# Relu-squared attention and a GELU MLP on one core: q and k rows in a ring of four groups, v in a ring of seven, PSUM tiles handed out by the kernel, a new order of the work

## The chip, the core and the metric

One NeuronCore of a Trainium2 chip. The metric is the device time of one execution in microseconds (us); lower is better. The kernel before takes 366.92 us (median of 3 runs, 366.43 to 367.38).

## What is computed

Eight batches of attention with 12 heads, 448 rows and 64 columns per head, and behind it an MLP on the 3584 rows of 768 columns that the heads make together. All arrays are float32 in memory; the kernel computes in bf16 and adds up in float32.

```python
scores = scale * np.matmul(q, k.transpose(0, 1, 3, 2))      # q, k, v: (8, 12, 448, 64)
attn = np.maximum(scores, 0.0) ** 2 / S
x = np.matmul(attn, v).transpose(0, 2, 1, 3).reshape(B * S, H * D)
h = x @ w_in                                                # (768, 2048)
g = 0.5 * h * (1.0 + erf(h * inv_sqrt2))
return g @ w_out                                            # (2048, 768)
```

## The kernel before, in words

**Attention.** The 12 heads of a batch are worked in 3 groups of 4. Rows of q and k (`nq`, `nk`) are loaded by DMAs that POOL (GpSimd) issues and that turn float32 into bf16. They are needed with the head's columns on the partitions (`qT`, `kT`). For batches 0 and 1 TensorE transposes them (`add_tk` L604, `add_tq` L631, into PSUM tiles `tp`, copied out by VectorE or ScalarE); for batches 2 to 7 SyncE (SP) issues transposing DMAs (`add_T_dma` L659), and a swap of the halves of `qT` is done by VectorE or by SP. The scores of two heads by 448 rows come in steps of four 64x64-tile matmuls into a PSUM tile `ps` (`fn_qk` L733, matmul L744); ScalarE (L756) or VectorE (L758) takes the relu, VectorE squares (L765), and after the steps of a group one AV product of 28 matmuls follows (`add_av`, L805, into `pav`), which is cast into `xT` (L518). Batch 0 is worked in two halves of the rows, so that its matmuls there are 224 wide.

**MLP.** `psh` is x @ w_in (L857, 6 matmuls for 128 of the 2048 columns), ScalarE takes the GELU into `h_sb`. The x @ w_in of the last four batches is done with seven block products instead of eight (`add_blocks`, `add_block`, `pb` L1009), from sums of the weights (`ws`) and of x that VectorE makes. h @ w_out is done by `add_plain` for the first tiles (L1295) and with seven products in the groups of 256 rows (`add_group`, `pso` L1191), from sums of w_out (`t_sb` L1120) and of h (`s_sb` L1170); VectorE adds the products up in `osb` (L1225), and SP stores.

**PSUM.** A pool `w_pp` of three tiles of two banks holds `ps`, `pav` and `pb` in turn, `f_pp` of two tiles of one bank holds `tp`, `psh`, `pso`. The pools rotate: a tile is given when the one that lay there, three (two) takes ago, is freed.

**Buffers for loads.** Batch 0 and batches from 2 on share one tile `nq` and one `nk` of 12 heads; batch 1 has its own. A load of group g of batch b waits for the transposes of group g of the batch before (`war` L542). v lies in three tiles of 12 heads; `xT` of batches 5 and 7 takes the place of a v tile.

**The order.** Nothing of the order is decided on the chip: each engine works its queue strictly in order. A `Scheduler` plans the queues ahead: the string `ORDER` (L86) names, by engine letter and number, which operation comes next on which engine (P TensorE, A ScalarE, D VectorE, G POOL, S SyncE; Z is a fill matmul on zeros), and the instructions are written in the order of the starts so planned. POOL's queue holds the loads; a load waits for one of eight DMA semaphores, so it also waits for the eighth load ahead of it. A small copy on POOL (`add_gate` L708) holds later loads back until a group's q (and, before, its k) is transposed. TensorE's queue starts with 11 matmuls on zeros (`spin`, L1369).

TensorE's work comes in three kinds by the shape in which it uses its array: whole-array products (psh, pso, pb, pse, spin: 128 x 128), 64x64 tiles (ps, pav, fill), and transposes (tp). A stretch of one kind without another in between is called a run.

Of the kernel before, what the change touches and what calls it, by code (L numbers as in the profile page):

```python
# [8 lines left out]
F32 = mybir.dt.float32  # L9
# [10 lines left out]
NA = 14  # L20
HP = H // 2
# [65 lines left out]
G0 G1 G3 G4 G1470 G7 A10 D13 A16 G121 P11 G2 P17 D12 D18 G117 P14 P42 D15 P39 G6 A43 P21 A40 P33  # L87
D22 P36 D44 P19 A37 P23 D20 G118 A34 D24 P25 G122 P54 D41 A26 G5 A55 P66 P57 Z1056 D67 A58 P63
P27 P29 A64 P69 D30 P48 D59 P31 A70 D28 D38 P78 A49 P51 D35 P133 G8 A52 D50 P45 D68 A79 P81 D53
A134 D46 P75 D47 G9 D65 A32 P131 A82 D56 P111 D132 A76 P108 D112 P129 G125 A109 D71 P102 P84 D103  # L90
G126 A85 P72 D80 P60 A73 D130 G120 A74 P93 D77 A61 P135 D104 A62 P96 D110 P105 A97 P141 D106 G147
A94 G124 D98 P165 A142 P90 P168 D107 A166 P143 D113 D86 A91 D83 P114 G119 A169 D92 P87 D115 A144
D95 A116 P171 D88 P137 A172 D89 P99 D138 A136 P159 P156 G128 D100 P145 D160 A157 D101 P162 A146
D173 P174 P186 G148 D175 P251 A187 D167 P243 A252 D170 A163 D158 P183 D188 A244 P189 P195 G150
P259 D184 A196 G154 A190 D176 P253 G151 D164 A260 G153 D161 P139 D191 P180 A140 P198 P177 D181
A199 D185 A254 P219 P216 G123 A178 P245 A220 G127 D179 S229 D182 P247 A246 A217 S228 P210 A248
P204 D218 P207 P263 A208 D205 P261 D211 A264 D197 S232 P192 A262 P213 D200 P222 A214 P255 D209
S231 A223 D193 P257 A256 D215 S235 P267 D206 A258 D194 S234 D221 P249 A268 D224 D212 P201 A250
P225 D230 G270 A202 A203 G238 P276 P279 A226 G149 D277 P265 A227 G239 A280 D233 P294 A266 P288
P291 A295 G152 P356 A289 P348 G272 G269 G271 P303 P285 A357 A292 A349 P350 A304 A286 P354 A351  # L100
D287 P312 P300 A355 P318 S399 P362 D281 D313 D296 P364 A363 D319 P370 D278 A301 A365 P358 A371
P315 P306 A359 P282 P352 D307 P360 A353 G241 P376 A361 P368 A377 A283 P366 A369 D284 D302 D236
D293 P372 A367 D290 P374 A373 P378 D390 D316 G274 P327 A379 P297 D391 A328 G273 G155 P333 P339
D314 A334 G240 P382 D298 D305 D317 A340 A375 S398 D308 A299 D320 D329 P330 P324 D417 P309 A325
P380 A383 A331 D310 D311 D392 P342 P321 P336 A381 A337 D332 D418 D341 D419 D326 S402 P384 A322
S401 D393 P387 D396 A385 S405 D394 D400 G407 G242 G237 A323 A343 G409 S386 G275 S404 P443 P446
D335 D420 G408 A444 P421 D395 D344 A447 D338 P449 D388 A450 D397 S389 A422 G412 P452 P345 D445
D346 P437 G411 P423 A453 A438 P440 A347 D424 D403 P455 S542 A441 P425 A456 D439 D442 P473 A426
P470 P461 P427 D454 A471 A474 D462 P429 D428 D457 P464 P479 P476 D430 A480 P431 D448 A465 D451
G414 G415 P433 D472 A477 D432 D562 D406 P467 P458 A468 S435 D469 P485 P491 S545 A486 D434 P509  # L110
D459 A492 S541 P513 A510 D560 A460 D478 D561 P503 S544 A514 P494 P500 D563 P519 A501 D481 D463
P515 A520 D475 A504 A495 D493 P517 D466 D543 S547 D496 D487 P488 A518 P482 A516 D502 S548 G552
P497 P511 D498 S436 G555 D499 P523 G551 A512 D489 A483 G550 A484 G416 P525 A524 D490 D546 G554
P600 G413 P609 P606 G410 D610 P521 D505 A601 A607 P603 P506 D604 A526 A522 P612 P639 D507 P531
A640 P527 G558 D613 D605 A532 D508 G557 P618 A528 P624 P615 D619 P529 S705 S704 A616 P537 S708
A530 A625 P535 A538 D620 D549 D626 D602 P627 P636 A536 P657 A637 P533 D611 D614 S707 A628 D608
D629 P539 A534 A658 P564 A540 D641 D659 D617 D638 P566 A565 P630 S710 S711 P633 P621 D631 A634
D632 S709 G715 P642 P651 A622 D635 P568 G718 G714 A623 D567 A652 G717 P570 G559 A569 D643 D706
P648 P666 P663 A649 P572 G721 A667 G722 D571 D644 D664 P660 P654 P645 G719 D661 A655 G716 G553
G556 D662 D650 G720 P769 P763 P574 A764 D573 D665 D668 A646 P576 A770 A647 D575 D580 S578 P772  # L120
P775 P778 P584 D577 S836 A776 A779 D656 D581 D653 D765 P586 S835 A585 A773 D777 P787 P766 D582
P669 A767 D587 A788 D712 P781 P588 A670 A671 D768 D780 D774 A782 D789 P790 P796 A791 P590 D783
D583 A797 D771 P799 A589 P784 S839 S842 A800 D591 P802 D801 P793 P592 D803 D785 A794 S838 P594
D593 D786 P596 D595 D837 P805 P811 D597 P823 A806 S841 P674 D792 A824 D795 D723 D798 P672 S843
D812 A675 P678 S598 D804 D807 P814 P817 P808 A815 D818 A673 D724 A679 P874 P820 A809 P676 D821
G849 D813 D825 P682 A677 G846 A875 G844 G851 P684 G847 A683 D840 G850 G845 A810 P829 A685 P880
G713 P826 G852 A830 P680 D827 D828 P688 A681 A881 D831 D816 D822 D819 P686 A689 P889 A687 P877
# [272 lines left out]
def kernel(  # L400
# [37 lines left out]
    def get_nat(b):  # L438
        if b not in nq:
# [11 lines left out]
            if b < 2:  # L451
                get_v(b)
# [1107 lines left out]
```

## Time and profile before

| | |
|---|---|
| runs | 366.43, 366.92, 367.38 us |
| span of the profiled execution | 365.2 us |
| TensorE (PE) busy | 356.2 us, 98% of the span |
| VectorE (DVE) busy | 297.5 us, 81% |
| ScalarE (ACT) busy | 208.2 us, 57% |
| POOL busy | 64.2 us, 18% |
| granted TensorE clock | 1.000 |

The span runs from the first to the last instruction in the trace; the run's time contains the start and the end around it, 366.92 - 365.2 = 1.7 us when the median is set beside this one span. In the rows of the timeline, a line has the start and the length in us, the engine, the line of the kernel, the operation with output and inputs, the shapes, and the count; what stands in brackets is idle time ahead of it and what ended it. In the chain of waits, a row has start, length, and what the end waited for.

### The profile page before, as it was taken

How to read it: one execution, taken by the hardware profiler on the slowest of the kernel's cores; microseconds unless marked ns; L12 is line 12 of the kernel's file. 1: busy time of each engine (PE TensorE's matmuls, PEld its weight loads, DVE VectorE, ACT ScalarE, POOL GpSimd, SP SyncE). 2: the span in 40 equal slices, each digit the busy share in tenths (PEclk: the TensorE clock that was granted, in tenths of full speed). 3: DMA queues.
4: the chain of work that ended last, by engine and by line, in shares of the span. 5: the costliest groups of instructions: out<-in, count | busy, mean ns of one | idle time of the engine just before them, and what ended most of it. 6: DMA issues, size and time to landing. Idle time of an engine off the chain costs nothing.

```text
span 365.2 us, 8578 instructions
## 1 busy us (share of the span) xinstructions
PE 356.2 (98%) x3598; PEld 225.4 (62%) x3598; DVE 297.5 (81%) x510; ACT 208.2 (57%) x337; POOL 64.2 (18%) x101
## 2 busy tenths in 40 slices
PE   8799999999999999999999999999999999999996
PEld 4575644455454445555445555799787689788664
DVE  3899784399999988999899999999867847665764
ACT  5998868555767686766766677437027024425310
POOL 8575224160124125014000000000000000000000
PEclk9999999999999999999999999999999999999999
DMA  9999999999999999999792301002021200140223
GB/s 168 199 200 207 198 154 138 191 203 181 186 221 198 197 172 209 219 157 154 132 168 70 95 20 43 3 2 86 3 85 46 88 0 2 45 129 2 85 70 106
DMA packets 73126, 44.12 MB, mean 121 GB/s; under 512 B 38144, under 2 KB 69760, under 8 KB 73088
## 3 DMA queue, kind: packets, MB, share of 16 engines
q0 software_dynamic: 32912, 22.47, 42.7%
q1 hardware_dynamic: 39280, 20.26, 29.0%
q10 hardware_dynamic: 896, 0.85, 0.7%
q8 instruction: 28, 0.46, 0.5%
q14 instruction: 10, 0.08, 0.1%
HBM read 45.61 MB, written 11.01 MB: 155 GB/s over the span
## 4 chain that ended last, share of the span: by engine, by line
PE 78%; DVE 10%; DMA 7%; POOL 2%; issue 2%; ACT 1%; POOLq 0%; DVEq 0%
PE pso L1191 33%; PE pb L1009 18%; PE psh L857 14%; PE ps L744 7%; PE pav L805 6%; DMA win_sb<-in_moe_w_in_dram 5%; DVE a_sq L765 4%; DMA nq<-in_q_dram 2%; DVE t_sb L1120 1%; DVE a_sq L758 1%; DVE s_sb L1170 1%; DVE qT L518 1%; POOL nk L553 1%; ACT a_sq L756 0%; POOL win_sb L481 0%
## 5 line engine op out<-in xcount | busy, mean ns | idle before, releaser
L756 ACT ACTIVATE a_sq<-ps 128x896 bf16<-128x896 f32 (+1 forms) x125 | 110.3, 927 | 33.5 <-PE ps L744 33.4
L765 DVE TENSOR_TENSOR a_sq<-a_sq 128x896 bf16<-128x896 bf16 (+1 forms) x169 | 96.9, 614 | 11.8 <-ACT a_sq L756 11.3
L857 PE MATMUL psh<-xT,win_sb 128*128 128x448 bf16 (+1 forms) x420 | 77.6, 337 | 0.9 <-DMA win_sb<-in_moe_w_in_dram 0.9
L857 PEld LDWEIGHTS <-win_sb 128*128 128x128 bf16 x420 | 38.9, 98 | 37.3 <-issue 9.4
L1046 DVE TENSOR_TENSOR part<-pb,part 128x448 f32<-128x448 f32 x80 | 47.3, 619 | 15.9 <-PE pb L1009 14.2
L1191 PEld LDWEIGHTS <-s_sb 128*128 128x128 bf16 x424 | 40.5, 98 | 26.8 <-issue 2.4
L758 DVE TENSOR_SCALAR a_sq<-ps 128x896 bf16<-128x896 f32 (+1 forms) x44 | 47.1, 1074 | 9.2 <-PE ps L744 9.1
L744 PE MATMUL ps<-qT,kT 64*64 64x448 bf16 (+1 forms) x756 | 47.7, 336 | 1.6 <-ACT qT L520 0.5
L867 ACT ACTIVATE h_sb<-psh 128x448 bf16<-128x448 f32 x64 | 35.0, 552 | 20.8 <-PE psh L857 20.4
L1191 PEld LDWEIGHTS <-h_sb 128*128 128x128 bf16 x312 | 29.4, 98 | 21.6 <-issue 4.6
L1009 PEld LDWEIGHTS <-win_sb 128*128 128x128 bf16 x384 | 36.8, 98 | 2.7 <-issue 0.4
L1191 PE MATMUL pso<-wout_sb,h_sb 128*128 128x384 bf16 x208 | 38.1, 326 | 0.0
L1191 PE MATMUL pso<-t_sb,s_sb 128*128 128x384 bf16 x208 | 38.1, 326 | 0.0
L1191 PE MATMUL pso<-wout_sb,s_sb 128*128 128x384 bf16 (+1 forms) x208 | 37.6, 324 | 0.0
L805 PE MATMUL pav<-a_sq,v_sb 64*64 64x448 bf16 (+1 forms) x756 | 36.7, 329 | 0.6 <-DVE a_sq L765 0.2
L1055 ACT ACTIVATE h_sb<-part 128x448 bf16<-128x448 f32 x48 | 25.4, 575 | 14.6 <-DVE part L1046 14.6
L1225 DVE TENSOR_TENSOR osb<-pso,p_sb 128x384 f32<-128x384 f32 x39 | 21.5, 552 | 14.7 <-PE pso L1191 11.0
L744 PEld LDWEIGHTS <-kT 64*64 64x64 bf16 x756 | 18.8, 105 | 22.3 <-issue 16.3
L805 PEld LDWEIGHTS <-v_sb 64*64 64x64 bf16 x756 | 21.4, 107 | 11.9 <-issue 2.5
L464 POOL DMA_DIRECT2D nq<-in_q_dram x24 | 17.8, 744 | 59.9 <-DMA qT<-nq 55.2
L1009 PEld LDWEIGHTS <-ws 128*128 128x128 bf16 x288 | 27.6, 98 | 1.0
L1055 ACT ACTIVATE h_sb<-pb 128x448 bf16<-128x448 f32 x16 | 8.2, 541 | 29.3 <-PE pb L1009 29.2
(62 smaller groups left out, 327.1 us busy)
## 6 DMA issues: line engine op xcount, KB each, us to landing
nk<-in_k_dram POOLq DMA_DIRECT2D x23, 224.0 KB, 8.1
nq<-in_q_dram POOLq DMA_DIRECT2D x21, 224.0 KB, 7.0
v_sb<-in_v_dram POOLq DMA_DIRECT2D x5, 672.0 KB, 11.6
out_dram<-osb SPq DMA_DIRECT2D x7, 336.0 KB, 2.9
v_sb<-in_v_dram POOLq DMA_DIRECT2D x9, 224.0 KB, 9.9
out_dram<-osb SPq DMA_DIRECT2D x7, 288.0 KB, 3.3
out_dram<-osb SPq DMA_DIRECT2D x8, 240.0 KB, 3.0
win_sb<-in_moe_w_in_dram POOLq DMA_DIRECT2D x8, 192.0 KB, 9.6
```

Of the source, the lines that this page charges most:

```text
L744: nc.tensor.matmul(ps[64 * j : 64 * j + 64, e, x * w : x * w + w], kT[r, g, i * 128 + 64 * j : i * 128 + 64 * j + 64], moving, start=True, ...
L756: A.activation(ar, ps, AF.Relu, scale=c_att)
L758: V.tensor_scalar(ar, ps, c_att, 0.0, op0=mybir.AluOpType.mult, op1=mybir.AluOpType.max,)
L765: V.tensor_mul(box["a2"][:, :, :used], ar, ar)
L805: nc.tensor.matmul(pav[0][o2 : o2 + 64, e, :w], vt[b][r, 2 * g + e, bass.ts(i, D)], box["a2"][r, y, o : o + w], start=(i == 0), stop=(i == ...
L857: nc.tensor.matmul(ph[:, x * n : x * n + n], win_sb[:, kd, bass.ts(m + x, 128)], xT[b][:, kd, c], start=(kd == 0), stop=(kd == KD - 1),)
L867: A.activation(h_ring()[:, m : m + nm, o + c.start : o + c.stop], box[0][:, :S].rearrange("p (x n) -> p x n", x=nm), AF.Gelu,)
L1009: nc.tensor.matmul(bank[name][:, y, z * HS : z * HS + HS], w[:, k, bass.ts(mm, 128)], right()[:, k], start=first and k == 0 and z == 0, st ...
L1046: V.tensor_add(get(to), ps(name), get(other))
L1055: A.activation(h_ring()[:, m : m + 2, o + half[c].start : o + half[c].stop], src().rearrange("p (x n) -> p x n", x=2), AF.Gelu,)
L1191: nc.tensor.matmul(box[bank][:, n0:n1], left()[:, kf], right()[:, kf, n0:n1], start=bool(need) and kf == 0, stop=kf == K2 - 1, skip_group_ ...
L1225: V.tensor_add(out()[:, n0:n1], box[bank][:, n0:n1], other()[:, n0:n1])
```

## The change

- **Rings.** The rows of q and k of batch 0 and of batches from 2 on lie in four slots of one group each (`nat_slot`), so that a load waits for the transposes of the group that lay in that slot, q and k each for their own (`war`). v lies in seven slots of one group (`VSLOTS`); `xT` of batches 5 and 7 takes three of these slots. Loads are issued by groups: the q load of 12 heads in batch 0 is three loads of four heads.
- **PSUM tiles.** A class `Banks` hands out the slots, first the one that was given back first; three double banks during attention, and from the first `pb` on (behind the last casts into `xT`) six single banks (`need=("u",)`), so that the block products take one bank each instead of half of a double one.
- **Batch 0.** The first group's q and k are laid so that one transpose turns two heads' rows (`pairs`): 11 transposes instead of 22.
- **Gates** wait for a group's q alone. v of batch 4 is loaded as two groups and one.
- **ORDER** is a new string, made by a planner that counts TensorE's instructions; the matmuls in all are the same except for these transposes. A fill of 1056 columns stands behind `spin`, where before one stood later. Counted in the order of TensorE's instructions, there are 123 runs before (52 whole-array, 60 of 64x64 tiles, 11 of transposes) and 108 after (46, 53, 9). The relus on VectorE are 43 up to the end of attention before and 48 after; the swaps on VectorE 26 and 22, and on SP 10 and 14.

The diff, cut to its core:

```diff
 KC = 112
...
+NN = 4
+NV = 7
+VSLOTS = ((0, 1, 2), (3, 4, 5), (6, 0, 1), (2, 3, 4), (5, 6, 3), (0, 1, 2), (4, 5, 6), (3, 4, 5))
+NW = 3
...
-G0 G1 G3 G4 G1470 G7 A10 D13 A16 G121 P11 G2 P17 D12 D18 G117 P14 P42 D15 P39 G6 A43 P21 A40 P33
...
+G1473 G7 A12 G0 A18 G1 G8 Z1056 G4 P13 D15 P16 D14 D17 P19 D20 G3 P35 D36 G9 P38 P29 A30 P21 D22
...
+class Banks:
+    def take(self, name, uses=1):
+        x = self.free.pop(0)
+        t = self.pool.tile(self.shape, F32, tag=f"w{self.n}_{x}", name=name)
+        self.left[id(t)], self.slot[id(t)] = uses, (x, t)
+        return t
+
+    def give(self, t):
+        self.left[id(t)] -= 1
+        if not self.left[id(t)]:
+            self.free.append(self.slot[id(t)][0])
...
+    def nat_slot(b, g):
+        return g if b < 2 else (3 * b + g + 1) % NN
...
-    def war(b, g0, g1):
-        c = {1: -1, 2: 0}.get(b, b - 1)
-        return [
-            o[0] for (bb, g, *_), o in list(Tq.items()) + list(Tk.items())
-            if bb == c and (b < 3 or g0 <= g < g1)
-        ]
+    def war(done, b, g0, g1):
+        old = []
+        for g in range(g0, g1):
+            if b == 1:
+                continue
+            for c, h in sorted({(x[0], x[1]) for x in done}, reverse=True):
+                if c != 1 and nat_slot(c, h) == nat_slot(b, g) and c != b:
+                    old += [o[0] for x, o in done.items() if x[:2] == (c, h)]
+                    break
+        return old
...
+            if pairs:
+                for i in range(i0, i1):
+                    nc.tensor.transpose(tp[:, bass.ts(i - i0, 128)], pairs_k()[:, i], ident)
+                return
...
-        deps = [Tq[b, g, 0][b == 2], Tk[b, g, 0][0]]
+        deps = [Tq[b, g, 0][b == 2]]
...
-                ps = box["ps"] = w_pp.tile([128, 2, NB], F32, tag="w", name="ps")
+                ps = box["ps"] = banks.take("ps")
...
-            pav.append(w_pp.tile([128, 2, NB], F32, tag="w", name="pav"))
+            pav.append(banks.take("pav", 2))
...
-                if first and name not in bank:
-                    bank[name] = w_pp.tile([128, 2, NB], F32, tag="w", name="pb")
+                if first:
+                    if banks.n == NW:
+                        banks.open(2 * NW, [128, NB])
+                    ps[name] = banks.take("pb")
...
-    add_q(0, 0, G, HC, NC)
+    for g in range(G):
+        add_q(0, g, g + 1, HC, NC)
...
-                add_v(b + 2, 0, G)
+                if b + 2 < B - 1:
+                    add_v(b + 2, 0, 2 if b == 2 else G)
+        if b == 3:
+            add_v(4, 2, G)
+        if b == B - 2:
+            add_v(B - 1, 0, G)
```

**TensorE, at the first h @ w_out products (`add_plain`).** Rows are single instructions: a weight load and the matmul that uses it. Before, this product stands behind score matmuls (`ps`), which are another kind:

```order
L744 LDWEIGHTS kT
L744 MATMUL ps<-qT,kT 64x448
L1295 LDWEIGHTS h_sb
L1295 MATMUL pso<-wout_sb,h_sb 128x384
L1295 LDWEIGHTS h_sb
```

After, the third product of this sort stands behind a `psh`, of the same kind:

```order
L939 LDWEIGHTS win_sb
L939 MATMUL psh<-xT,win_sb 128x448
L1374 LDWEIGHTS h_sb
L1374 MATMUL pso<-wout_sb,h_sb 128x384
L1374 LDWEIGHTS h_sb
```

Before, each of the four plain products has score or AV matmuls on both sides; after, two stand in a run by themselves, one joins a run of psh, and one joins another.

**VectorE, at the end of batch 0's attention.** `a_sq` is the relu or its square, `xT` the cast of an AV product, `kT` and `qT` copies of transposed rows. Before (L765 square, L758 relu, L518 copy or cast):

```order
L758 TENSOR_SCALAR a_sq<-ps 128x896
L765 TENSOR_TENSOR a_sq<-a_sq 128x896 x2
L765 TENSOR_TENSOR a_sq<-a_sq 128x2x224
L765 TENSOR_TENSOR a_sq<-a_sq 128x896 x3
L518 CAST xT<-pav 128x224
L765 TENSOR_TENSOR a_sq<-a_sq 128x896
L518 CAST xT<-pav 128x224 x2
L518 COPY kT<-tp 128x896
L518 CAST xT<-pav 128x224
```

After (L840 square, L832 relu, L565 copy or cast):

```order
L565 COPY qT<-tp 128x896
L565 COPY kT<-tp 128x896
L840 TENSOR_TENSOR a_sq<-a_sq 128x896 x7
L832 TENSOR_SCALAR a_sq<-ps 128x896
L840 TENSOR_TENSOR a_sq<-a_sq 128x896
L840 TENSOR_TENSOR a_sq<-a_sq 128x2x224
L565 COPY qT<-tp 128x896
L565 COPY kT<-tp 128x896
L565 CAST xT<-pav 128x224 x2
```

A cast that stood ahead of the last squares now stands behind them, a relu stands between them instead of ahead, and the copies of batch 1's transposed rows stand on both sides.

**POOL, around the loads of w_out.** Rows are loads (DMA, with the tile's shape) and gates (COPY). Before:

```order
L464 DMA nq<-in_q_dram 112x4x256
L487 DMA wout_sb<-in_moe_w_out_dram 128x16x384
L571 DMA v_sb<-in_v_dram 128x2x448
L487 DMA wout_sb<-in_moe_w_out_dram 128x4x384 x2
L571 DMA v_sb<-in_v_dram 128x2x448
L464 DMA nq<-in_q_dram 112x4x256
L553 DMA nk<-in_k_dram 128x2x448 x2
L487 DMA wout_sb<-in_moe_w_out_dram 128x4x384 x2
```

After:

```order
L786 COPY gate<-qT 128x16
L622 DMA v_sb<-in_v_dram 128x2x448
L604 DMA nk<-in_k_dram 128x2x448
L622 DMA v_sb<-in_v_dram 128x2x448
L513 DMA nq<-in_q_dram 112x4x256
L786 COPY gate<-qT 128x16
L513 DMA nq<-in_q_dram 112x4x256
L534 DMA wout_sb<-in_moe_w_out_dram 128x16x384
L534 DMA wout_sb<-in_moe_w_out_dram 128x4x384 x4
L513 DMA nq<-in_q_dram 112x4x256
```

The five loads of w_out stood between loads of q, k and v with no gate ahead; they now stand together, behind two gates and more loads.

363 lines of the change are left out of this document (202 added, 161 removed).

## The prediction

> **What bounds the kernel now.** I read the page first, then the busy time by stage.
>
> ```profile
> PE 356.2 (98%) x3598; PEld 225.4 (62%) x3598; DVE 297.5 (81%) x510; ACT 208.2 (57%) x337; POOL 64.2 (18%) x101
> PE   8799999999999999999999999999999999999996
> DVE  3899784399999988999899999999867847665764
> PEclk9999999999999999999999999999999999999999
> ```
>
> TensorE (PE) is busy in 98% of the span of 365.2 us, at full clock in every slice. VectorE (DVE) is the next, and in slices 8 to 30 it reads 8 or 9 as well. By stages (columns: the stretch, its length, then busy us and instructions of PE, weight loads, DVE, ACT, POOL, then the clock):
>
> ```profile
> 0.00:38.00 38.00, 32.84 (x624) 21.40 (x624) 30.81 (x60) 30.73 (x45) 25.96 (x41) 1.00 1.25 193
> 38.00:120.00 82.00, 81.77 (x776) 42.25 (x774) 65.21 (x106) 57.22 (x89) 24.22 (x37) 1.00 1.31 187
> 120.00:229.00 109.00, 108.87 (x1085) 56.20 (x1084) 102.25 (x169) 75.15 (x113) 14.03 (x24) 1.00 0.82 134
> 229.00:365.20 136.20, 132.75 (x1119) 105.53 (x1117) 99.26 (x178) 45.09 (x92) 0.00 (x0) 1.00 0.17 50
> ```
>
> From 38 to 229 us these rows leave TensorE 0.36 us idle (0.9 by the closer reading below), so little waiting is left there to be taken away; the 3.45 us of the last stretch lie almost all behind the last product, at 361.75. What isn't work lies in the first 38 us (5.2 us idle). The waits of TensorE, longest first (us in total, times, longest):
>
> ```profile
> PE spin L1369 <- DVE zero L1352: 1.0, 1, 1.0
> PE psh L857 <- DMA win_sb<-in_moe_w_in_dram: 0.9, 2, 0.5
> PE tp L640 <- DMA nq<-in_q_dram: 0.8, 1, 0.8
> PE ps L744 <- ACT a_sq L756: 0.4, 1, 0.4
> PE pav L805 <- DVE a_sq L765: 0.2, 1, 0.2
> ```
>
> So a gain must come from the start, or from TensorE's work itself. The number of matmul columns is the same in both kernels except for eleven paired transposes, so only what a change of the kind of work costs can shrink.
>
> **The change, part by part.** *Fewer changes of kind.* TensorE works in runs of one kind: whole-array products (psh, pso, pb), 64x64 attention tiles (ps, pav), transposes (tp). Counted from both instruction orders there are 123 runs before (52, 60 and 11) and 108 after (46, 53 and 9). What a run costs beyond its matmuls shows in the chain of waits, where these rows follow each other without a gap (start, us, instructions):
>
> ```profile
> 43.32 0.69 PE ps L744 x12
> 47.08 4.65 PE psh L857 x24
> 59.19 0.50 PE ps L744 x8
> 59.69 2.38 PE psh L857 x12
> ```
>
> Two runs of 12 psh take 4.76, one of 24 takes 4.65: 0.11 for a run. Four ps cost 0.69 - 0.50 = 0.19, so twelve cost 0.57 and their run 0.12. For transposes I take 0.13, near the ps. That gives 6 x 0.11 + 7 x 0.12 + 2 x 0.13 = **-1.8 us** (-1.6 to -2.0 for 0.11 to 0.13 on all). Nothing hides it, as TensorE has no idle time there.
>
> [...]
>
> *The start.* I measure it by TensorE's lag: the clock at an instruction less all the TensorE work ahead of it, counted at the rates above (runs included). The last load that it waited for sets the lag for all that follows:
>
> ```profile
> 4.54 7.03 DMA nq<-in_q_dram
> 25.35 10.47 DMA win_sb<-in_moe_w_in_dram
> 35.96 2.24 PE L857 MATMUL psh<-xT,win_sb 128*128 128x448 bf16 x11 [0.49 <-DMA win_sb<-in_moe_w_in_dram]
> 53.29 1.47 SPq L667 DMA_TRANSPOSE kT<-nk  x1
> 4.30 0.23 POOL ident L1356
> ```
>
> At 35.96 there are 25.9 us of work behind it: lag 10.0, and counted in the same way it is larger by at most 1 us anywhere later. Reading the loads in POOL's order (float32 at the source), 2.75 MB had landed at 11.57 and 12.06 MB at 35.82: 0.384 MB/us. In the new order win_sb comes earlier against its use; the tightest load is v of batch 1, 15.47 MB deep, due at work position 37.4. It lands at 35.82 + 3.41/0.384 = 44.7, so it asks for a lag of 7.3, or 8.7 with one transposing DMA in between, which holds SP's queue for 1.3 to 1.5 us, as in this row. The loads would allow -1.3 us.
>
> VectorE allows less. Its part of batch 0:
>
> ```profile
> 4.99 0.78 DVE L518 CAST nk<-k 128x512 bf16<-128x512 f32 x1 [3.97 <-DMA k<-in_k_dram]
> 7.60 0.39 DVE L518 COPY qT<-tp 128x448 bf16<-128x448 bf16 x1 [0.42 <-PE tp L640]
> 27.55 0.61 DVE L765 TENSOR_TENSOR a_sq<-a_sq 128x896 bf16<-128x896 bf16 x1
> 28.08 0.68 DVE L518 CAST xT<-pav 128x224 bf16<-128x224 f32 x2
> 28.68 0.61 DVE L518 COPY kT<-tp 128x896 bf16<-128x896 bf16 x1
> 29.59 1.08 DVE L758 TENSOR_SCALAR a_sq<-ps 128x896 bf16<-128x896 f32 x1
> 28.36 0.86 PE L805 MATMUL pav<-a_sq,v_sb 64*64 64x224 bf16 x28
> ```
>
> The last square of batch 0 ends at 28.16 and its AV starts 0.2 later: from 4.99 that is 20.4 us of work and 2.7 us lost. Ahead of that square the new order has two more relus (+2.0), one more kT copy (+0.6), one qT copy less (-0.3; 0.39 with overlap) and three xT casts less (-1.0): 21.7 us. Its AV stands at work position 18.7. With nothing lost VectorE ends at 26.7, lag 8.1 with the step to TensorE; with the same 2.7 lost, 10.8. I take half of that loss, as the squares now stand in longer unbroken rows (seven where there were three): 9.5, so **-0.5 us** (-1.3 to +0.8). The fill of 0.4 us behind the spin matmuls stands where TensorE waits for its first rows anyway and is within this; without that cover it costs its 0.4. POOL makes the identity (0.23) ahead of its first loads instead of behind four of them, which puts these back by no more and is within the range too. Pairing the first transposes takes 11 of them from a stretch in which TensorE waits for inputs: nothing.
>
> *The rings.* Rows of q and k come free by groups, v by groups, and POOL's gates wait for q alone. In the trace of before loads are awaited by TensorE only in the first 36 us, so earlier loads beyond that bring nothing, 0. Later loads can cost. The one that stands later is w_out, now behind a second gate:
>
> ```profile
> 52.11 0.73 POOL L464 DMA_DIRECT2D nq<-in_q_dram  x1 [10.45 <-DMA qT<-nq]
> 52.84 1.16 POOL L487 DMA_DIRECT2D wout_sb<-in_moe_w_out_dram  x1
> 71.22 0.76 POOL L487 DMA_DIRECT2D wout_sb<-in_moe_w_out_dram  x1 [12.16 <-DMA wout_sb<-in_moe_w_out_dram]
> 79.23 1.96 PE L1295 MATMUL pso<-wout_sb,h_sb 128*128 128x384 bf16 x11
> ```
>
> The first w_out tile lands 18.4 us after its issue and 8 us before its use. After, that use is at position 66.3 plus lag 9.5, 75.8. The gate's swap on VectorE has 44.3 us of VectorE work ahead of it, so the issue is at about 53, with up to 2.3 MB of loads still ahead: 53 + 18.4 = 71.4 with none of them left, 77.4 with all at 0.384. I take the middle, 74.4: no wait, **0**.
>
> *Batches 2 to 7.* VectorE gets five more relus from ACT there, less four swaps that SP takes: +1.6 us net up to the last AV, which stands at position 213.6 instead of 222.1. Its idle time from 38 to 229, 23.5 us by the stages above, shrinks to about 14. The PSUM tiles that the kernel hands out first-freed-first cannot wait longer than a fixed rotation, and the trace has hardly a wait for one. What the trace shows of waits there:
>
> ```profile
> 39.22 1.32 PE pav L805 x28
> 94.78 0.54 PE L805 MATMUL pav<-a_sq,v_sb 64*64 64x448 bf16 x5
> 95.55 1.32 PE L805 MATMUL pav<-a_sq,v_sb 64*64 64x448 bf16 x23 [0.23 <-DVE a_sq L765]
> 122.97 0.38 PE L744 MATMUL ps<-qT,kT 64*64 64x448 bf16 x4
> 123.49 1.52 PE L805 MATMUL pav<-a_sq,v_sb 64*64 64x448 bf16 x28
> ```
>
> 28 AV matmuls take 1.32, 0.047 each. The five from 94.78 have till 95.55, so 0.53 is lost there; the four ps at 122.97 need 0.19 and have 0.52, so 0.33 is lost: 0.9 together. That can go, -0.9, or grow; upwards I bound it by one such 0.53 at every fourth of the 18 AVs, +2.4. I take **0**: VectorE's room shrinks, but its relus are spread otherwise, and no row weighs the one against the other.
>
> *The last stage.* The same products, from single PSUM banks of which six are there instead of three pairs; without idle before, so 0. The last tile on VectorE is 256 wide instead of 128:
>
> ```profile
> 361.34 0.42 DVE L1225 TENSOR_TENSOR osb<-pso,osb 128x256 f32<-128x256 f32 x1 [0.32 <-PE pso L1191]
> 361.79 0.29 DVE L1225 TENSOR_TENSOR osb<-pse,osb 128x128 f32<-128x128 f32 x1
> ```
>
> 0.42 for 0.29: **+0.1** (-0.1 to +0.2).
>
> *Sum:* -1.8 - 0.5 + 0 + 0 + 0.1 = -2.2, so a span of 363.0. The runs shown have a median of 366.92, 1.7 us above the profiled span (start and last store); I keep those 1.7: **364.7 us**. With all ends best (-2.0, -1.3, -0.9, -0.1) 362.6, with all worst (-1.6, +0.8, +2.4, +0.2) 368.7.
>
> **The rivals.** *VectorE takes the bound in batches 2 to 7.* It works strictly in order; each relu moved to it stands ahead of squares that an AV waits for. From 120 to 229 us it is busy 102.25 of 109 already, and after it has some 9 us less room. Against it: before, it held up only two places in spite of this. The forecast's gain of 2.2 is gone at 2.2/18 = 0.12 us for each AV. At 0.3 each, a little over half of the 0.53 seen at 95 us, 5.4 us of waits stand where 0.9 were: 364.7 + 4.5 = **369.2, slower**.
>
> *w_out lands late.* If all 2.3 MB are still ahead, the wait is 77.4 - 75.8 = 1.6; if they move slower, as 134 GB/s from 120 to 229 us stands to 193 in the first 38 (0.267 MB/us), they take 8.6, so 80.0 and a wait of 4.2. Middle 2.9: **367.6**, with its cases evenly from 366.3 to 368.9, a third of them above 368.0. For it: the first tile took 18.4 us. Against it: 8 us of slack before.
>
> *The changes of kind are saved, but the start gives them back.* VectorE loses as much as before (+0.8) and waits in attention grow by 1 us: -1.8 + 0.8 + 1.0 + 0.1 = 0.1, **367.0**. For it: nearly all VectorE slices of the start are 8 or 9. That would be the change not doing what it counts on.
>
> **How the numbers follow.** A measurement of this kernel can tell about 0.3%, 1.1 us, from no change, so faster means below 365.8 and slower above 368.0. Forecast 0.58, VectorE bound 0.14, w_out late 0.14, start gives it back 0.14. Faster 0.58; same 0.14 + 0.09 = 0.23; slower 0.14 + 0.05 = 0.19. The range reaches from near the best end, 362.9, over the third rival and most of the second to 368.4; left out are the first rival and the last part of the second, under 2 in 10.
>
> **What would show it.** Right: the same rows of ps and psh per run, 15 runs fewer, TensorE busy 1.8 us less, a win_sb or v wait (if any) at a lag of 9 to 10 by 45 us, a last product ending near 359.6. Wrong: waits of pav on a_sq at many of the 18 AVs; a wait of pso on wout_sb near 76; a lag above 10.5 at 45 us. [...]

## The result, and the profile after

The changed kernel takes **371.09 us** (median of 6 runs, 369.87 to 374.33); the kernel before, beside it on the same chip, 366.35 us (6 runs, 365.95 to 367.38). The ratio is **1.014** (95%: 1.011 to 1.017): slower, where 364.7 was forecast, and above the range. The profiled execution, the shortest of the six, took 369.87 us with a span of 368.1, 2.9 us more than the span of before. One execution each of the experiments 1, 4 and 15 was slow throughout (1484.8, 383.58 and 372.03 us) and is left out of the medians and ratios below, and of the trace of 4 only the rows shown are used.

The page of the changed kernel: busy totals, then two of its rows by slices.

```profile
PE 357.2 (97%) x3587; PEld 227.4 (62%) x3587; DVE 303.9 (83%) x518; ACT 199.1 (54%) x325; POOL 65.8 (18%) x104
PE   8799999999979999999999999999999999999995
PEclk9999999999998999999999999999999999999999
```

Each slice is 9.2 us. TensorE has one hole that was not there before, in the slice from 101 to 110 us, and the clock dips in the slice behind it. The stages (same columns as in the prediction) place it:

```profile
0.00:38.00 38.00, 33.52 (x635) 21.92 (x636) 29.79 (x56) 30.21 (x49) 27.13 (x43) 1.00 1.26 191
38.00:120.00 82.00, 79.53 (x734) 41.53 (x733) 68.21 (x107) 48.98 (x76) 20.53 (x32) 0.98 1.30 187
120.00:229.00 109.00, 109.00 (x1098) 56.98 (x1094) 104.23 (x174) 77.52 (x116) 18.13 (x29) 1.00 0.84 139
```

From 38 to 120 us TensorE is idle for 2.47 us (0.23 before) and its clock is 0.98; from 120 to 229 us it isn't idle at all, though VectorE is busy 104.23 of 109. The waits of TensorE say for what it was idle:

```profile
PE pav L880 <- DMA v_sb<-in_v_dram: 2.5, 1, 2.5
PE ps L818 <- ACT a_sq L830: 1.0, 3, 0.5
```

One wait of an AV product for its rows of v. TensorE's timeline around it, and a stretch of the same work a little later:

```profile
106.86 0.57 PE L818 MATMUL ps<-qT,kT 64*64 64x448 bf16 x8
109.89 2.12 PE L880 MATMUL pav<-a_sq,v_sb 64*64 64x448 bf16 x28 [2.47 <-DMA v_sb<-in_v_dram]
111.80 0.97 PE L818 MATMUL ps<-qT,kT 64*64 64x448 bf16 x8
112.69 1.97 PE L939 MATMUL psh<-xT,win_sb 128*128 128x448 bf16 x6
114.60 0.76 PE L818 MATMUL ps<-qT,kT 64*64 64x448 bf16 x12
...
119.20 1.49 PE L880 MATMUL pav<-a_sq,v_sb 64*64 64x448 bf16 x28
120.53 0.55 PE L818 MATMUL ps<-qT,kT 64*64 64x448 bf16 x8
121.01 1.31 PE L939 MATMUL psh<-xT,win_sb 128*128 128x448 bf16 x6
```

From start to start, the 28 AV matmuls take 1.91 us after the wait and 1.33 later, the eight scores 0.89 and 0.48, the six psh 1.91 where twelve took 2.38 in the prediction's rows, 1.19 for six. So work that comes *after* the wait is slow: some 1.7 us on top of the 2.47. Windows of 4 us show why (busy times, then clock, DMA share, GB/s):

```profile
104.00:108.00 4.00, 3.43 (x26) 1.61 (x23) 3.38 (x7) 2.00 (x3) 0.00 (x0) 1.00 1.34 176
108.00:112.00 4.00, 2.10 (x32) 1.25 (x36) 1.28 (x2) 0.64 (x2) 0.00 (x0) 0.83 1.28 180
112.00:116.00 4.00, 4.00 (x33) 1.36 (x23) 3.19 (x5) 2.91 (x5) 0.00 (x0) 0.74 1.25 231
```

Halved for 0.17 x 4 x 2 = 1.4 us in the one window and 0.26 x 4 x 2 = 2.1 in the next: one piece of 3.4 us at half clock (0.50 in each microsecond from 111 to 114), which costs half of it, 1.7.

**Where the load came from.** The v that is awaited is that of batch 3. Its load, on POOL's timeline (in brackets, what POOL waited for):

```profile
58.75 4.16 POOL L534 DMA_DIRECT2D wout_sb<-in_moe_w_out_dram  x5 [0.73 <-issue]
62.86 0.75 POOL L513 DMA_DIRECT2D nq<-in_q_dram  x1
...
94.82 0.71 POOL L513 DMA_DIRECT2D nq<-in_q_dram  x1 [11.96 <-DMA qT<-nq]
...
97.27 0.84 POOL L622 DMA_DIRECT2D v_sb<-in_v_dram  x1
```

SP's timeline, and the chain of waits:

```profile
64.71 22.83 SPq L741 DMA_TRANSPOSE qT<-nq  x3
```

```profile
97.27 12.59 DMA v_sb<-in_v_dram
```

Before, on POOL, the same load:

```profile
80.79 0.84 POOL L571 DMA_DIRECT2D v_sb<-in_v_dram  x1
```

This is read backwards. v of batch 3 is issued at 97.27, 16.5 us later than before, and takes 12.6. Ahead of it in POOL's queue stands q of batch 5, group 0, which waited 12 us: it goes into the ring slot of q of batch 3, group 2, whose transpose hadn't landed. That transpose is the third of the row on SP that holds its queue for 22.83 us, till 87.5: its rows were issued (62.86) right behind all of w_out, 2048 x 768 x 4 bytes = 6.29 MB, at the prediction's 0.384 MB/us 16.4 us of loading.

### The profile page after: what moved, and what is told of

Its sections match the earlier page's. It is cut to its first block, busy times and chain, and to the rows that moved or that the text cites. A ratio compares the mean times of both kernels' runs of the same rounds, so it can differ in the third digit from the quotient of the medians.

```text
span 368.1 us, 8588 instructions
## 1 busy us (share of the span) xinstructions
PE 357.2 (97%) x3587; PEld 227.4 (62%) x3587; DVE 303.9 (83%) x518; ACT 199.1 (54%) x325; POOL 65.8 (18%) x104
## 4 chain that ended last, share of the span: by engine, by line
PE 90%; DVE 4%; DMA 3%; issue 1%; ACT 1%; POOL 0%; DVEq 0%
PE pso L1268 30%; PE psh L939 20%; PE pb L1091 18%; PE ps L818 9%; PE pav L880 9%; DMA v_sb<-in_v_dram 3%; PE pso L1374 2%; DVE a_sq L840 1%; PE spin L1448 1%; DVE a_sq L832 1%; PE tp L714 0%; DVE s_sb L1247 0%; DVE qT L565 0%; DVE kT L565 0%; PE tp L679 0%
## 5 line engine op out<-in xcount | busy, mean ns | idle before, releaser
L830 ACT ACTIVATE a_sq<-ps 128x896 bf16<-128x896 f32 (+1 forms) x120 | 105.5, 923 | 30.7 <-PE ps L818 30.3
L840 DVE TENSOR_TENSOR a_sq<-a_sq 128x896 bf16<-128x896 bf16 (+1 forms) x169 | 97.4, 618 | 3.5 <-ACT a_sq L830 3.0
L939 PE MATMUL psh<-xT,win_sb 128*128 128x448 bf16 (+1 forms) x420 | 78.6, 339 | 0.0
L832 DVE TENSOR_SCALAR a_sq<-ps 128x896 bf16<-128x896 f32 (+1 forms) x49 | 52.6, 1079 | 11.6 <-PE ps L818 11.2
L1122 DVE TENSOR_TENSOR part<-pb,part 128x448 f32<-128x448 f32 x80 | 47.0, 620 | 16.4 <-PE pb L1091 16.3
L604 POOL DMA_DIRECT2D nk<-in_k_dram x23 | 16.5, 720 | 38.8 <-DMA kT<-nk 24.0
L1091 PE MATMUL pb<-xs,ws 128*128 128x224 bf16 x192 | 22.8, 259 | 0.0
## 6 DMA issues: line engine op xcount, KB each, us to landing
v_sb<-in_v_dram POOLq DMA_DIRECT2D x4, 672.0 KB, 11.1
```

The costliest lines, as they stand in the source:

```text
L830: A.activation(ar, ps, AF.Relu, scale=c_att)
L832: V.tensor_scalar(ar, ps, c_att, 0.0, op0=mybir.AluOpType.mult, op1=mybir.AluOpType.max,)
L840: V.tensor_mul(box["a2"][:, :, :used], ar, ar)
L939: nc.tensor.matmul(ph[:, x * n : x * n + n], win_sb[:, kd, bass.ts(m + x, 128)], xT[b][:, kd, c], start=(kd == 0), stop=(kd == KD - 1),)
L1091: nc.tensor.matmul(ps[name][:, z * HS : z * HS + HS], w[:, k, bass.ts(mm, 128)], right()[:, k], start=first and k == 0 and z == 0, stop=k ...
L1122: V.tensor_add(get(to), ps[name][:, :S], get(other))
```

## The experiments

The balance of the two spans: work -1.8, as forecast; lag (clock less TensorE's work ahead) behind the start 10.1 to 10.5, +0.4; the late v and the half clock, 2.47 and 1.7 by the rows above, +4.2; the end behind the last product +0.5. What is left of the 2.9, -0.4, is put down to the rest of attention. (The medians differ by 4.7; the profile is of the shortest execution.) Open was why v was late: its *place* in the queue, what stands ahead of it, or that all loads are due too early for the DMA engines. Order words below: G277 is the load of v of batch 3; G272, G276 are q of batch 3 in groups 0 and 2, G273 and G275 its k in groups 1 and 2; G410 is k and G414 q of batch 4; G157 is v of batch 2, group 2.

**1 and 5. v of batch 3 ahead** of the ring's waiting load, tried twice.

```diff
-G414 G412 ... S547 G277 P475
+G414 G277 G412 ... S547 P475
```

> The changed kernel with one word of ORDER moved: the load of v of batch 3 stands in POOL's queue ahead of a gate and of the q load that waits for a transposing DMA, instead of behind them (issue near 82 us instead of 97). Theory: the changed kernel loses 2.5 us because this load is issued too late, and about 1.7 us more because TensorE's clock is halved for 3.4 us behind that idle time; so here the wait is gone, the clock is 1.000, the lag stays near 10.5 up to the AV of batch 3, and the time is near 365.5 (ratio 0.998 to the kernel before). Rival A: the load is slow because the DMA engines are crowded, not because it is issued late; then it lands later than 12.6 us after its issue and part of the wait stays, 368 or more. Rival B: the next load in the queue becomes late in its place, 367 to 369.

> The same kernel as in the run e1_v3_early, for a profile: the profiled execution there took four times as long in every part and shows no waits, while the timed ones (370.4 to 371.8) show no gain. Theory, changed by that: the DMA engines are busy through the whole stretch up to 140 us and the data of batch 3 as a whole come too late, so that with v moved ahead another load or a transposing DMA of batch 3 is waited for, again about 2 to 3 us with the clock halved behind it, between 85 and 125 us. Rival: the wait moved to a place that has nothing to do with DMAs (VectorE's order, a PSUM tile).

Measured: 371.27 and 371.31 us, ratios 1.014 (1.012 to 1.016) and 1.015 (1.012 to 1.017): no gain. The longest wait in the second's trace, and its chain of waits:

```profile
PE ps L818 <- DMA qT<-qT: 2.9, 1, 2.9
```

```profile
62.91 25.19 DMA nq<-in_q_dram
...
88.12 1.22 SPq L741
...
89.43 3.90 SPq L741
...
93.43 7.36 DMA qT<-qT
```

v is in time, and now the scores of batch 3, group 1, wait 2.9 us for the swap of their q, with the half clock behind it again (0.58 in the window from 100 to 104). Read in order, the chain says why: q of group 2 lands 25 us after its issue behind w_out; SP, in order, stands at its transpose; then come a transpose of k and only then the swap of group 1, which takes 7.4 us. The wait has moved, so v's place alone isn't the cause.

**2. The late v in the kernel before.** Order word of this load there: G275.

```diff
-S386 G275 S404 ... G412 P452
+S386 S404 ... G412 G275 P452
```

> The kernel before with the same load moved the other way: behind the k and q loads of batch 4 that wait for transposing DMAs (issue near 97 instead of 81), nothing else changed. Theory: it lands at about 109 where its AV is due at 107.3, so a wait of about 2 us appears, the clock falls behind it, and the time is 366.4 + 2 + 1.7 = 370. Rival: the loss of the changed kernel comes from its rings, PSUM tiles or order of TensorE; then this edit costs less than 1 us.

Measured: 366.39 us, ratio 1.0005 (0.999 to 1.002). Nothing waited for the load. How long it took to land, and the first AV product of batch 3:

```profile
DMA to landing us min/median/max: 11.8/11.8/11.8
```

```profile
107.38 1.49 PE L805 MATMUL pav<-a_sq,v_sb 64*64 64x448 bf16 x28
```

It was issued at 94.68, so it landed at 106.5, 0.9 us ahead of its use. The edit did not make the load late, and so it tells nothing of what a late v costs in the order of before. TensorE asks for this v at the same time in both orders: at 107.3 before, and at 109.89 - 2.47 = 107.4 after. What it asks for sooner are rows of q and k: counted along its order, the first scores of batch 3 start at 82.3 us after the change and at 92.5 before.

**3. The wait filled** with twelve matmuls on zeros ahead of the AV product that waits.

```diff
             pav.append(banks.take("pav", 2))
+            if (b, g) == (3, 0):
+                for _ in range(12):
+                    nc.tensor.matmul(
+                        pav[0][:D, 0, :NB], zero[:D, :D],
+                        zero[:D, :1].to_broadcast([D, NB]), start=True, stop=True
+                    )
```

> The changed kernel with 12 matmuls on zeros (512 columns, 64x64, 2.56 us of work) written into the PSUM tile of the first AV of batch 3 ahead of that AV, so that TensorE works where it had been idle for 2.47 us; the result is not touched. Theory: the idle time is what halves the clock; the clock stays at 1.000 and the time is 1.7 us shorter than the changed kernel's, profiled about 368.2, and the runs scatter less. Rival: the clock falls for another reason (the load on the chip after the stall); then the clock is near 0.993 again and the time near 370.

Measured: 369.12 us (368.36 to 373.41), ratio 1.011 (1.005 to 1.017). The medians differ by 2.0 us, but the intervals overlap; the trace is plainer:

```profile
107.75 2.34 PE L875 MATMUL pav<-zero 64*64 64x512 bf16 x10
109.80 0.38 PE L886 MATMUL pav<-a_sq,v_sb 64*64 64x448 bf16 x3
```

```profile
108.00:112.00 4.00, 4.00 (x48) 2.13 (x46) 1.77 (x3) 1.17 (x3) 0.00 (x0) 1.00 1.25 194
112.00:116.00 4.00, 4.00 (x30) 1.89 (x29) 3.71 (x6) 3.63 (x7) 0.00 (x0) 1.00 1.22 255
```

v is as late as after the change (AV at 109.80), but the clock stays at 1.00. From the start of the eight scores ahead of the wait to that of the eight scores behind the next AV product, TensorE takes 13.67 us after the change (106.86 to 120.53), 12.01 here (107.35 to 119.36), and 9.49 in experiment 13, which has no wait. So this place costs 4.2 us after the change and 2.5 with the wait filled. The half clock is a price of its own for the idle time.

**4. The price of a change of kind**: in the kernel before, one 64x64-tile matmul of 16 columns ahead of each of 48 block products, which makes 48 more pairs of runs.

```diff
+                if first:
+                    nc.tensor.matmul(
+                        bank[name][:D, y, :16], zero[:D, :D],
+                        zero[:D, :1].to_broadcast([D, 16]), start=True, stop=True
+                    )
                 for z, m in enumerate(ms):
                     w, mm = left(m)
```

> The kernel before with one matmul of 16 columns in a 64x64 tile ahead of each of the 48 first products of the block products in the last stage, into the PSUM tile that the product then overwrites: 48 more runs of 64x64 tiles and 48 more whole-array runs. Theory: by the rows of the prediction a pair of runs costs 0.11 + 0.12 = 0.23 us, so +11 us, and up to +1.5 for the small matmuls themselves: 377.5 to 379. [...]

Measured: 377.54 us, ratio 1.030 (1.028 to 1.032), so +11.1 us (10.4 to 11.9), 0.23 for a pair of runs, the small matmul itself included. The timeline agrees:

```profile
251.10 1.31 PE L1014 MATMUL pb<-xT,win_sb 128*128 128x224 bf16 x12
252.25 0.74 PE L1014 MATMUL pb<-xT,ws 128*128 128x224 bf16 x6
...
254.06 0.19 PE L1007 MATMUL pb<-zero 64*64 64x16 bf16 x1
...
254.87 0.19 PE L1007 MATMUL pb<-zero 64*64 64x16 bf16 x1
```

Six pb take (252.25 - 251.10) / 2 = 0.575; with a switch in and out they take 254.87 - 254.06 = 0.81, so 0.235.

**6. Loads of batch 4 behind those of batch 2 and 3**: G157, then G277, then G410.

```diff
-G273 D324 G410 D402 ... G157 D340 ... S547 G277 P475
+G273 D324 D402 ... G157 G277 G410 D340 ... S547 P475
```

> The changed kernel with the load of v of batch 3 moved further ahead, directly behind the last load of batch 2, and the first load of k of batch 4 moved behind it: in POOL's queue nothing of batch 4 stands ahead of batch 3 any more. Theory (DMA capacity up to 110 us is used up, and what the ring of q and k lets run ahead takes it from batch 3): the waits of batch 3 shrink by what 0.46 MB take, 1.2 us, and the time falls to 368 to 369. Rival (the wait is for the transposing DMAs, which are slow by themselves): no gain, 370 to 372.

Measured: 371.82 us, ratio 1.015 (1.013 to 1.018). The swap of batch 3's q is awaited for 3.1 us, and the clock is 0.84 and 0.73 in the two windows of 4 us from 100 to 108: as in 5.

**7 and 8. q of batch 3, group 2, ahead of w_out**, alone, and together with 1.

```diff
-G272 D295 ... D333 G276 P323
+G272 G276 D295 ... D333 P323
```

> The changed kernel with one word of ORDER moved: the q load of batch 3, group 2, stands in POOL's queue ahead of the five loads of w_out (6.3 MB) instead of behind them. Theory: that load lands 25 us after its issue because it is behind w_out on the DMA queues; SP, in order, waits for it with a transposing DMA (19.7 us), everything of batch 3 on SP and, on POOL, the q load of batch 5 (same slot of the ring) and behind it v of batch 3 come late by that. Then with this one edit q lands before 72, v of batch 3 is issued before 90, no wait of TensorE over 0.7 us is left between 85 and 125, the clock is not halved there, and the time is 365.5 to 366.8. Rival: the DMA engines' capacity is the limit, so w_out or another load becomes late by as much: 368.5 or more.

> The edit of e7_q3_ahead_of_wout and that of e1_v3_early together. Theory: nothing more to gain than e7, within 0.5 us of it, 365.5 to 366.8. Rival (v is late in e7 too): this one is faster than e7 by 1 us or more. Second rival (capacity): a later wait for w_out or a transposing DMA, 368.5 or more.

Measured: 369.51 us, ratio 1.010 (1.007 to 1.012), and 370.60, 1.012 (1.008 to 1.016). The two longest waits of the first in attention and the MLP:

```profile
PE pso L1268 <- DVE osb L1302: 1.2, 1, 1.2
...
PE ps L818 <- DMA qT<-qT: 0.7, 1, 0.7
```

No load is awaited for longer than 0.7, and the run's clock is 1.000; the 1.2 is a product held up by VectorE's add, which waits 1.85 us for a store of `osb` to land. With v early too, the swap is late by 2.1 again, and the run's clock is 0.994. The loads of this stretch trade places.

**9. The swap of batch 3, group 1, on VectorE** instead of SP, with v early.

```diff
-G414 G412 P386 S405
+G414 G277 G412 P386 D405
```

> The kernel of e1_v3_early with the swap of qT of batch 3, group 1, on VectorE (two copies of 64 x 896) instead of two DMAs from SP. Theory: the swap waited on SP behind transposing DMAs and then 7.4 us for its own landing; on VectorE it is ready by about 94, ahead of its use at 98, so the wait of 2.9 and the half-speed clock behind it go away: 366.5 to 367.5, with perhaps 0.5 to 1 of waits for w_out and q left. Rival: VectorE is held by the swap's wait for the transposed q (its queue is in order) and the squares behind it come late: 369 or more.

Measured: 369.97 us, ratio 1.011 (1.007 to 1.014). Now others are late, with the run's clock at 1.000:

```profile
PE pso L1374 <- DMA wout_sb<-in_moe_w_out_dram: 2.2, 1, 2.2
...
PE ps L818 <- DMA kT<-nk: 1.2, 1, 1.2
```

**10. The last tile**: 7 with the last products in the order of before, so that the last sum is 128 wide.

```diff
-P1464 D1462 D1466 S1445 P1460 S1467 D1461 P1463 S1468 S1471 S1469 D1465 S1470
+D1462 S1445 P1460 S1467 D1461 P1463 P1464 S1468 S1469 D1465 D1466 S1470 S1471
```

> The edit of e7_q3_ahead_of_wout, and the last three products of the last group in the order of the kernel before: the product of 128 columns last, its add and its store behind those of 256 columns. Theory: from the end of the last product to the end of the span the changed kernel takes 3.9 us where before took 3.5, from the wider add (0.42 for 0.29) and the wider store; so this one is 0.3 to 0.5 us faster than e7. Rival: the order of the stores on the queue decides, no difference.

Measured: 371.99 us (368.52 to 373.72), ratio 1.015 (1.008 to 1.022), so wide that it settles nothing; its profile, of the shortest of its runs, has a span of 366.8, that of 7 has 366.9. The traces say more: from the end of the last product to the end of the span it is 3.5 us before (361.75 to 365.2), 3.9 after (364.18 to 368.1), and still 3.9 here (362.91 to 366.8) and in 15 (361.30 to 365.2), which has this order too. So the order of the last products is not what makes the end longer; what does stays open.

**11 and 12. The rows of batch 3 between w_out's pieces, and all of them ahead of w_out.**

```diff
-G272 ... G240 A377 ... D333 G276 P323 ... G273 D324 G410 D402 ... G157 D340
+G272 ... G240 G276 G273 A377 ... D333 P323 ... D324 D402 ... G157 G410 D340
```

> The changed kernel with POOL's queue turned so that q of batch 3 group 2 and k of group 1 stand behind the first load of w_out (3.1 MB, the half of the columns that the first products use) and ahead of its other four (3.1 MB), and the first k load of batch 4 behind the last load of batch 2. Theory: what is late is set by the place of the six loads of w_out's two halves ahead of batch 3's rows, and the DMA engines have just enough capacity: the rows land before 80, SP's transposes and the swap of group 1 are done by 90, POOL's q load of batch 5 and v of batch 3 come before 90, the second half of w_out lands before 86; no wait over 0.7 us and no half clock between 85 and 125, time 365.5 to 366.8. Rival (capacity is exceeded): a wait of 1 to 2.5 us for w_out near 86, or again for the swap near 98; 368 to 370.

> The changed kernel with all rows of batch 3 (q of group 2, k of groups 1 and 2) ahead of the five loads of w_out. Theory as in e11: batch 3 is not waited for at all, but the first product with w_out at 76.9 waits for 1.4 MB more in front of it, 2 to 3 us, and the clock is halved behind that: 368 to 370. Rival (only the rows of batch 3 matter, w_out has slack): 365.5 to 366.8.

Measured: 368.48 us, ratio 1.007 (1.004 to 1.009), and 373.44, 1.019 (1.017 to 1.022). TensorE's wait for w_out, of 11 and of 12:

```profile
PE pso L1374 <- DMA wout_sb<-in_moe_w_out_dram: 2.3, 2, 1.4
```

```profile
83.22 7.89 PE L1374 MATMUL pso<-wout_sb,h_sb 128*128 128x384 bf16 x32 [5.90 <-DMA wout_sb<-in_moe_w_out_dram]
```

In 11 it comes in two pieces, 0.9 and 1.4, with the clock at 1.000 and no other wait in this stretch: the best division of the lateness without any change of TensorE's order, and still 2.3 us of it. In 12 all of it is on w_out (in brackets), and the windows show the clock halved for 6.8 us:

```profile
80.00:84.00 4.00, 0.78 (x3) 0.40 (x3) 0.49 (x1) 0.00 (x0) 0.21 (x1) 0.70 1.28 191
84.00:88.00 4.00, 4.00 (x15) 1.79 (x13) 0.00 (x0) 0.00 (x0) 0.00 (x0) 0.50 1.28 190
88.00:92.00 4.00, 4.00 (x32) 2.08 (x31) 3.46 (x6) 0.81 (x2) 2.46 (x5) 0.95 1.28 195
```

Part of the half clock lies inside the wait (from 80 to 84 us TensorE is busy for 0.78 only), so it costs less than its half: the 32 products take 7.89 us, where they take 5.37 in the timeline of after.

**13 and 14. Bytes taken away**: the changed kernel without the load of v of batch 3, and 11 without v of two groups of batch 2.

```diff
             x = 2 * v_slot(b, g0)
+            if b == 3:
+                return
             nc.gpsimd.dma_start(
```

> The changed kernel without the load of v of batch 3 (1.4 MB); the AV products of batch 3 then multiply the rows of v that lay in these slots before, so batch 3's part of the output is another. Theory: the changed kernel's order of TensorE is not slower by itself; with the one load gone that it waits for, its waits between 85 and 125 us are under 0.7 and the clock is full there: 371.1 - 4.4 = 366.5 or less (365.3 to 366.8). Rival: the loss has other parts that the wait hides, 368 or more.

> The kernel of e11_rows3_between_wout without the loads of v of batch 2, groups 1 and 2 (0.9 MB, one ahead of w_out, one behind it); the AV products of these groups then multiply old rows of v, so their part of the output is another. Theory (capacity): by about 90 us the DMA engines are 2.3 us behind what this order asks for, and 0.9 MB are 2.4 us at 0.384 MB/us; so the wait for w_out near 86 to 90 shrinks from 2.3 to below 1 and the time falls by 1.4 to 2.3, to 366.2 to 367.1. Rival (w_out is late by its place in the queues, not by the bytes ahead): the wait stays above 1.8 and the time near 368.5.

Measured, in 10 runs each: 366.37 us, ratio 0.9985 (0.9965 to 1.0006), and 366.54, 0.9995 (0.997 to 1.002). The first's timeline at the place of the wait:

```profile
107.46 0.57 PE L820 MATMUL ps<-qT,kT 64*64 64x448 bf16 x8
107.86 1.59 PE L882 MATMUL pav<-a_sq,v_sb 64*64 64x448 bf16 x28
...
116.95 0.55 PE L820 MATMUL ps<-qT,kT 64*64 64x448 bf16 x8
```

No wait and full clock: 1.38 MB less (3.6 us at 0.384 MB/us), and 371.09 - 366.37 = 4.7 us are back. As 13 takes away the very load that is waited for, it shows what the wait costs, not why the load is late. That is what 14 tests: 0.92 MB that nothing waited for are gone (2.4 us), which brings 368.48 - 366.54 = 1.9 us, and the wait for w_out, another load, is 1.2 instead of 2.3 (below 1 was expected; the profile is of the longest of its runs). So the bytes that are due set much of the lateness. They do not set all of it: the loads behind the missing ones also move up in 14, and the same bytes in other places gave longest waits for a load or a swap from 0.7 us (7) to 5.9 (12).

**15. w_out asked for later**: 11 with one h @ w_out product behind a psh, with the quarters of w_out used in the order in which they land, and with the tail of 10.

```diff
-P386 S405 ... A387 G554 ... P368 ... A369 P389
+S405 ... G554 ... P368 P386 ... A369 A387 P389
...
-            for kf in range(KF):
+            for kf in (0, 1, 2, 3, 8, 9, 10, 11, 4, 5, 6, 7, 12, 13, 14, 15):
```

> The kernel of e11_rows3_between_wout with the use of w_out's second half put later instead of its loads earlier: its first product (add_plain, first tile, left half) stands behind one more psh, and add_plain goes through the rows of w_out in the order of its four loads; the last three products in the order of the kernel before (128 columns last). Theory: the two waits of 0.9 and 1.4 us shrink to 0.5 in all, and the end is 0.3 to 0.4 shorter: 368.5 - 1.8 - 0.4 = 366.3 (365.8 to 367.0), about the kernel before. Rival: the second halves of the sums of w_out on VectorE come as late as before and the products of the group behind wait for them: 367.5 to 368.5.

Measured: 368.23 us (11 runs, 365.89 to 370.38), ratio 1.004 (1.001 to 1.007). Its profiled execution has no wait for w_out and the span of before, 365.2, so the later use does take the wait away; but the runs scatter over 4.5 us, and it doesn't beat the kernel before. None of the versions does. The trace has one more thing, a half clock near the start:

```profile
16.00:24.00 8.00, 6.44 (x166) 5.18 (x158) 6.47 (x12) 6.64 (x13) 6.54 (x10) 0.79 1.39 197
```

That is 0.21 x 8 x 2 = 3.4 us at half clock, where no wait of TensorE's is longer than 0.54 us. The traces of 6 (from 8 to 16 us; the run's clock is 0.989) and 14 (from 18 to 26; 0.993) have the same 0.79 there.

## Why the prediction was wrong

**The step that failed** is the one on the rings: "The one that stands later is w_out", costed at 0 because its first tile would land ahead of its first use. That much came true: the chain of waits after has

```profile
76.89 5.31 PE pso L1374 x32
```

with no wait ahead of it. What was not priced is what stands *behind* w_out. "Later loads can cost" was followed for the use of one tile alone, not for the loads queued behind it, for SP, which transposes in order (its queue held for 22.83 us above), and for POOL, whose next load waits for a ring slot (12 us). And TensorE's new order asks for the first rows of q and k of batch 3 10 us sooner (82.3 against 92.5), while the DMA engines already moved 183 GB/s at a share of 1.29; v of batch 3 is due at the same time as before, and is issued 16.5 us later. The same stretch before and after:

```profile
52.00:90.00 38.00, 38.00 (x348) 19.13 (x337) 25.46 (x40) 24.11 (x41) 14.60 (x21) 1.00 1.29 183
```

```profile
52.00:90.00 38.00, 38.00 (x340) 19.20 (x339) 32.60 (x50) 23.47 (x37) 12.87 (x19) 1.00 1.29 183
```

The same 183 GB/s and the same share: nothing loads faster after the change, while some rows are due sooner and the load of v is issued later. In place of this step's 0 the runs show 2.5 us of waiting for that v and 1.7 us of half clock behind it. The rival "w_out lands late" had the right stretch and the right kind of resource, but its price hung on w_out itself; moving the rows ahead of w_out (12) makes exactly that rival true.

**The half clock** was in no term: 1.7 us behind a wait of 2.5. A piece of 3.4 us came behind waits of 2.5, 2.9 and 3.1 us (after, 5, 6), and 8, with a wait of 2.1, has a clock of 0.994, about that of 5 with its one piece (0.995). A wait of 2.2 (9) and two of 0.9 and 1.4 (11) brought none: the clock is 1.000 in both. And in the first 26 us of 6, 14 and 15 a piece came, and since the first microsecond no wait had been longer than 0.7. So the length of the wait alone does not tell it here, and the runs do not show what does.

**Fewer changes of kind, -1.8: the price is right.** 4 gives 0.23 for a pair of runs, 11.1 us for 48, where the forecast's rows gave 0.11 and 0.12. That all of the 1.8 came is worked out from this price and the count, not measured by itself. The sign that the prediction named for it, TensorE busy for 1.8 us less, did not come: 357.2 us, of which 1.7 are the half clock, and 356.1 in 13 at full clock, against 356.2. By 38 us TensorE has done 1.0 us less work in 13 than before (the start, below), and yet it reads 33.5 us busy there against 32.8; so busy time is no clean measure of work in that stretch.

**The start, -0.5 forecast: +0.4 measured**, inside its bounds (in 13 it is +1.0, outside them). VectorE's and TensorE's rows after:

```profile
27.63 0.92 DVE L840 TENSOR_TENSOR a_sq<-a_sq 128x896 bf16<-128x896 bf16 x2
```

```profile
5.36 0.64 PE L1612 MATMUL fill<-zero 64*64 64x512 bf16 x3
5.93 0.37 PE L707 MATMUL tp<-ident,nq 112*128 112x112 bf16 x4
```

The last square of batch 0 ends at 28.55, against 26.7 with nothing lost and 29.4 with the old loss: the half was taken, two thirds were lost. And the fill did not stand in idle time: the first transposes start at 5.93, behind its end, where they started at 5.42 before.

**VectorE doesn't become the bound**: waits of TensorE for `a_sq` are some 1.4 us in all, and from 120 to 229 us it is never idle. The forecast's 0 for batches 2 to 7 came out as -0.4, within its bounds.

**The tail, +0.1 forecast, +0.5 measured**: from the last matmul's start to the span's end 4.2 us instead of 3.7. Only the add was priced. 10 and 15 have the narrow add of before again, and the time behind their last product stays at 3.9, so the forecast's reason isn't what made the end longer.

**What the change would bring without the late load** is shown by 13: 0.9985, -0.6 us (-1.3 to +0.2), no more than a measurement can just tell. There the balance is work -1.8, start +1.0, the rest of attention -0.3, tail +0.5. So of the rivals, "the start gives them back" comes nearest to the change with its loads in time (367.0 against 366.4), by its start and not by the waits in attention, which it had growing; the late load makes the loss on top.

**What stays open**: what makes the end longer; when an idle time brings the half clock, and what brings it near the start; why the runs of 10 and 15 scatter. In 10 the runs carry their clock with them (368.52 us at 0.998, 370.35 at 0.994, 373.64 and 373.72 at 0.991), so pieces at half clock that come or don't may be part of it. That isn't shown: runs of the kernel before took 366.63 us at 0.994 and 366.43 at 1.000.

## What to carry to other kernels

When a block of loads is moved ahead of others, price what stands behind it on every queue that is worked in order (POOL's loads, which here landed in the order of their issue, all 84 in the trace of after; the engine that turns the rows; the engine whose next load waits for a slot), not the block's own use; and set the bytes due by each time against the rate, since here, with 183 GB/s moving before and after, another place mostly chose which load was late, and in the worst place made it later (12, 5.9 us). A saving of TensorE's work that makes it ask for rows sooner is worth only what the loads allow: take bytes away in one experiment to see which of the two it is. Of five TensorE waits of 2.1 to 3.1 us here, three had the clock halved behind them and a fourth stood in an execution with a clock of 0.994; the one of 2.5 cost 1.7 us beyond its length, so divide such a wait (11: 1.000) or fill it (3: 1.00).

## What the runs showed of the hardware

- A change of TensorE's kind of work and back, with one matmul of 16 columns between, costs 0.23 us, 11.1 us for 48 of them.
- Behind TensorE waits of 2.5, 2.9 and 3.1 us the clock was halved for a piece of 3.4 us, which cost 1.7 us behind the wait of 2.5; with a wait of 2.1 us the execution's clock was 0.994, with one of 2.2 us 1.000. With the wait of 2.5 filled by matmuls on zeros the clock stayed at 1.00. At a wait of 5.9 us it was halved for 6.8 us, in part within the wait, and the products behind took 2.5 us longer.
- A piece of 3.4 us at half clock also came within the first 26 us of three executions (0.79 over 8 us each), where since the first microsecond no wait had been longer than 0.7.
- At a DMA share of about 1.3 a load of 0.46 MB of rows issued behind 6.3 MB took 25 us to land, and a swap of `qT` within the chip 7.4 us, where the page of after has a median of 2.6.
